# Loading the rows for block sums: one transfer over 96 partitions and one over 24, instead of four over 24

## The chip, the cores and the metric

The kernel runs on one core of one Trainium2 chip. The metric is the device time of one execution in microseconds (us), lower is better. The five engines are named as in the profile: PE (matrix multiplication), DVE (vector), ACT (scalar, activation), POOL (GpSimd) and SP (which only issues transfers and waits). All transfers between HBM and SBUF are carried by 16 DMA engines; SP and ACT issue theirs on hardware queues (q1 and q10 in the profile), POOL on a software queue (q0).

## The reference

Two layers one after the other, for 4 batches, 8 heads, 768 positions and 64 numbers a head, all in fp32.

```python
# layer 1: sparse attention (block=32, window=16)
k_sum = k.reshape(B, H, 24, 32, D).max(axis=3)
v_sum = v.reshape(B, H, 24, 32, D).mean(axis=3)      # the block sums of this case
scores = concat(local scores within the window, q.k_sum + log(32))
attn   = softmax(scores) @ concat([v, v_sum], axis=2)
# layer 2: mixture of 4 attention experts over x = attn in (B, S, 512)
w = softmax over the 2 best of x @ w_gate
out = sum over experts of w_e * (causal_attention(x wq_e, x wk_e, x wv_e) @ wo_e)
```

What matters here is `v_sum`: for every head, 24 sums of 32 consecutive rows of 64 numbers.

## The kernel before

The work is cut into batches `b` (0 to 3) and, inside a batch, into two groups `g` of four heads and four pairs `c` of two heads. Layer 1 works pair by pair (`stage1_pair`): transposes of q and k on PE, scores, an exponential on ACT (tile `aT`), the product with `vb` on PE (L437), division and transposes. Layer 2 (`stage2`) follows for each batch: projections (L630 with `wqk`, L554 with `wvg`), causal scores (L654), an exponential on ACT (L662, tile `a`), masking of the diagonal on POOL (L667), the product with v on PE (L678), and the output product (L734) with its stores (L745).

The order of the work is written out by hand: a table lists each step with its engine and its buffers, and every engine runs its steps strictly in that order. Neither the order nor the buffers change here.

The rows of v come to the core twice. The step `load_v` (SP, L284 to L287, four transfers a pair) lays the rows out in `vb`, 64 rows a tile, for the product. The block sums come in two ways. Three of the eight (batch, group) sets use PE (L304). The other five, (1,1), (2,0), (2,1), (3,0) and (3,1), use the function `tree`:

- Step `dvs` loads the rows of four heads into the tile `vt`, of which there is **one** buffer. Head j goes to partitions 32j to 32j+23: each partition holds one block of 32 rows, 2048 numbers, 8 KB, in one piece. These are four transfers on SP (L339), each 24 partitions by 8 KB.
- Two steps `tr` add on POOL (L347), in place: 2048 columns to 1024, then 512, 256, 128 and last 64 into the tile `vu`, over partitions 0 to 119. That is five additions for a set.
- Steps `ds` copy the sums from `vu` into `vb` (L170, by POOL).

Because `vt` has one buffer, the next set's load waits until POOL has made the last addition of the set before (SP's wait at L339 for `vu`). POOL's queue holds, behind the additions, the masks of layer 2 (L667) and the issues of the loads of k and q (L261, L266, tiles `kn` and `qn`), so whatever holds up an addition holds up these too. SP's queue holds, behind a `vt` load, the weights (L501, L507, L512; only behind the first), the `vb` loads and the output stores.

Each transfer on SP tells of its end by one of eight semaphores taken in turn, so a transfer isn't issued before the one eight places ahead has landed.

Of the kernel before, what the change touches and what calls it, by code (L numbers as in the profile page):

```python
# [7 lines left out]
FP32 = mybir.dt.float32  # L8
HALF = mybir.dt.float16
AL = mybir.AluOpType  # L10
# [5 lines left out]
S = 768  # L16
D = 64
# [5 lines left out]
NSUM = 24  # L23
# [135 lines left out]
def make_plan(nc, T, q, k, v, moe_w_gate, moe_wq, moe_wk, moe_wv, moe_wo, out):  # L159
# [3 lines left out]
    def en(e):  # L163
        return getattr(nc, ENG[e])

    def copy(e, dst, src):
        if e == "A":
            nc.scalar.copy(dst, src)  # L168
        else:
            en(e).tensor_copy(dst, src)  # L170
# [163 lines left out]
    def tree(b, g):  # L334
        t, u = R.buf("vt"), R.buf("vu")

        def load(e):
            for j in range(4):
                nc.sync.dma_start(out=T["vt"][t.slot][32 * j:32 * j + NSUM, :],  # L339
                                  in_=v[b, 4 * g + j].rearrange("(n s) d -> n (s d)", s=32))  # L340
        R.step(f"dvs{b}{g}", {"S": 1.8}, [vtz], [t], load, dma=3.0)
        for i, ws in enumerate(((1024,), (512, 256, 128, 64))):
            def add(e, ws=ws):
                x = T["vt"][t.slot]
                for w in ws:
                    y = T["vu"][u.slot] if w == 64 else x[:, 0:w]
                    en(e).tensor_tensor(y[0:120], x[0:120, 0:w], x[0:120, w:2 * w], AL.add)  # L347
            R.step(f"tr{b}{g}{i}", {"G": sum(0.13 + w * 0.00218 for w in ws)}, [t],
                   [u] if i else [t], add, keep=[t])
        for c in (2 * g, 2 * g + 1):  # L350
            def dsum(e, c=c):
                for h in range(2):
                    j = 32 * (2 * (c % 2) + h)
                    copy(e, T["vb"][vb[b, c].slot][WIN:KR, 12 * h:12 * h + 12, 0:64],
                         T["vu"][u.slot][j:j + NSUM, :].unsqueeze(1).to_broadcast((NSUM, NQ, 64)))
            R.step(f"ds{b}{c}", {"G": 1.75, "V": 0.95, "A": 1.64}, [u], [vb[b, c]], dsum)
# [403 lines left out]
    for i in range(24):  # L760
        fb, n = R.buf("ps"), 4 if i < 8 else 1
# [37 lines left out]
def decode(text):  # L799
    out = []  # L800
    for w in text.split():
        i, e, s = w.split(",")
        out.append((int(i) if i != "f" else -1, e, [int(x) for x in s.split(".") if x]))
    return out


@with_exitstack
def kernel(
    ctx: ExitStack,
    tc: tile.TileContext,  # L810
    q, k, v,
    moe_w_gate, moe_wq, moe_wk, moe_wv, moe_wo,
    out,
):
    nc = tc.nc
    ctx.enter_context(tc.manual_schedule())
    sb = ctx.enter_context(tc.tile_pool(name="sb", bufs=1))
    ps = ctx.enter_context(tc.tile_pool(name="ps", bufs=1, space=bass.MemoryType.PSUM))
    T = {}

    def one(name, shape, dt):
        T[name] = sb.tile(shape, dt, name=name)

    def many(name, shape, dt):
        T[name] = [sb.tile(shape, dt, name=f"{name}{i}") for i in range(SLOTS[name])]

    one("zz", (128, 512), HALF)
    one("w1", (128, 1), FP32)
    one("w1b", (128, 1), FP32)
    one("id16", (128, 128), HALF)  # L830
    one("idr", (KP, KP), HALF)
    one("id32", (128, 128), FP32)
    one("mt", (128, 128), HALF)
    one("pi", (128, 6, 64), HALF)
    one("wqk", (128, 2, NCH, 2, 128), HALF)
    one("wvg", (128, NCH, 264), HALF)
    one("wo", (128, 2, 512), HALF)
    one("wg32", (128, NCH, 4), FP32)
    one("wgt", (128, NCH, 4), FP32)
    many("qn", (128, 4, 384), HALF)  # L840
    one("sel", (96, 56), FP32)
    many("kn", (KP, 4, 512), HALF)
    many("ks", (128, NSUM), HALF)
    many("kw", (128, NQ, 128), HALF)
    many("qT", (128, S), HALF)
    many("aT", (128, 2, 384), FP32)
    many("x32", (128, S), FP32)
    many("vb", (128, 24, 65), FP32)
    many("vs", (128, 2, 128), FP32)
    many("vt", (128, 2048), FP32)  # L850
    many("vu", (128, 64), FP32)
    many("rec", (128, 2, NT, 1), FP32)
    many("hi", (128, S), HALF)
    many("lo", (128, S), HALF)
    many("v2", (128, NT, E, 65), HALF)
    many("lgp", (128, NT, 4), FP32)
    many("gt", (128, 6, NT, 4), FP32)
    many("qk", (128, S), HALF)
    many("a2", (128, 5376), HALF)
    many("cmb", (128, 2, NT, 1), FP32)  # L860
    many("wav", (128, NT, 128), HALF)
    many("wT", (128, S), HALF)
    one("ob", (128, SLOTS["ob"], 512), FP32)
    T["ps"] = ps.tile((128, 8, 512), FP32, name="ps")
    T["ps16"] = T["ps"].bitcast(HALF)

    R = make_plan(nc, T, q, k, v, moe_w_gate, moe_wq, moe_wk, moe_wv, moe_wo, out)
    R.emit(decode(TABLE))
# [30 lines left out]
```

## Time and profile before

| | us |
|---|---|
| median of 3 runs | 167.77 (167.38 to 168.11) |
| the profiled execution | 168.57 |
| its span, first to last instruction | 166.7 |

The profile covers the one execution of 168.57 us; 1.9 us of it lie outside the span. Its page gives busy time by engine, a row of digits for 40 slices of the span, the DMA queues, the chain of work that ended last, groups of instructions, and the transfers by the line that issued them. Times in views are us from the start of the span. A bracket at the end of a timeline row tells how long the engine was idle before it and what ended that. In the view by stretches (windows), the last three numbers are the granted PE clock as a fraction, the mean busy share of the 16 DMA engines (it can exceed 1, as packets overlap) and GB/s.

### The profile page before, as it was taken

The numbers are of one execution on the slowest core, as the hardware profiler recorded it, in microseconds if no ns is written. First come the engines' busy times: TensorE is split into PE (matmuls) and PEld (weight loads), VectorE is DVE, ScalarE is ACT, GpSimd is POOL, SyncE is SP. The second block draws the span as 40 slices with busy tenths as digits, with TensorE's granted clock in tenths as the row PEclk, the third lists the DMA queues.
The fourth block names the chain that finished last, engine by engine and source line by source line (L and its number), as shares of the span: only waits on it lengthen the run. The fifth ranks groups of instructions, "written<-read, shape, count | busy, mean of one in ns | idle before, by whom it ended". The sixth has DMA issues, their size and how long they took to land.

```text
span 166.7 us, 6783 instructions
## 1 busy us (share of the span) xinstructions
PE 144.8 (87%) x2903; PEld 107.5 (64%) x2903; DVE 114.7 (69%) x235; ACT 123.9 (74%) x159; POOL 111.5 (67%) x181
## 2 busy tenths in 40 slices
PE   0259798996899979995999989999999999999993
PEld 0246676873677757684757878766678795477551
DVE  5074389869586885964986879993974797247840
ACT  3048976998499968996779877797877874997630
POOL 7988699628998588799699999716999130315000
DMA  3999999999988996999798958998400000200572
GB/s 28 170 215 227 217 209 155 233 215 166 174 212 174 135 202 135 167 186 179 178 142 117 257 102 222 200 219 294 175 4 6 0 4 4 114 11 22 231 283 102
DMA packets 44302, 25.35 MB, mean 152 GB/s; under 512 B 33168, under 2 KB 40592, under 8 KB 43792
## 3 DMA queue, kind: packets, MB, share of 16 engines
q1 hardware_dynamic: 35840, 17.96, 48.2%
q0 software_dynamic: 7488, 6.29, 25.7%
q10 hardware_dynamic: 944, 0.66, 1.2%
q8 instruction: 23, 0.38, 1.1%
q14 instruction: 7, 0.06, 0.1%
HBM read 24.91 MB, written 6.29 MB: 187 GB/s over the span
## 4 chain that ended last, share of the span: by engine, by line
PE 48%; DMA 20%; DVE 11%; ACT 6%; issue 6%; POOL 5%; SPq 2%; POOLq 0%; DVEq 0%; ACTq 0%
DMA qn<-in_q_dram 9%; PE ps L437 9%; PE ps L630 6%; DMA out_dram<-ob 6%; DMA kn<-in_k_dram 5%; PE ps L554 5%; PE ps L366 4%; PE ps L734 4%; PE ps L678 4%; PE ps L654 4%; PE ps L304 3%; PE ps L766 3%; PE ps L414 2%; ACT a L662 2%; DVE x L452 2%
## 5 line engine op out<-in xcount | busy, mean ns | idle before, releaser
L662 ACT ACTIVATE a<-ps 128x1024 f16<-128x1024 f32 (+1 forms) x48 | 42.2, 921 | 7.2 <-PE ps L654 6.0
L667 POOL TENSOR_SCALAR_AFFINE_SELECT a<-a 128x256 f16<-128x256 f16 x48 | 18.7, 408 | 20.8 <-ACT a L662 20.1
L427 ACT ACTIVATE aT<-ps 120x768 f32<-120x768 f32 x32 | 25.3, 817 | 6.8 <-PE ps L420 6.7
L437 PE MATMUL ps<-vb,aT 120*64 120x65 f32 x768 | 26.5, 224 | 1.3 <-issue 0.7
L347 POOL TENSOR_TENSOR vt<-vt 120x1024 f32<-120x1024 f32 (+3 forms) x20 | 24.0, 1202 | 4.9 <-DMA vt<-in_v_dram 3.8
L437 PEld LDWEIGHTS ps<-vb,aT 120*64 120x64 f32 x768 | 24.1, 138 | 4.3 <-issue 2.3
L630 PE MATMUL ps<-hi,wqk 128*128 128x384 f16 x128 | 23.1, 326 | 2.2 <-issue 1.9
L630 PEld LDWEIGHTS <-wqk 128*128 128x128 f16 x128 | 11.9, 98 | 10.8 <-issue 2.9
L170 POOL COPY vb<-vb 32x1408 f32<-32x1408 f32 x10 | 13.4, 1350 | 6.0 <-PE ps L734 4.4
L482 DVE TENSOR_TENSOR lo<-ps,hi 128x768 f16<-128x768 f32 x16 | 15.2, 955 | 2.9 <-ACT hi L168 2.4
L170 POOL COPY vb<-vu 24x768 f32<-24x768 f32 x20 | 16.5, 823 | 1.1
L366 PE MATMUL ps<-idr,kn 100*64 100x100 f16 x256 | 8.9, 219 | 9.4 <-POOL kn L219 7.4
L452 DVE TENSOR_TENSOR x<-ps,rec 128x768 f32<-128x768 f32 x16 | 15.3, 958 | 0.6
L382 DVE TENSOR_REDUCE ks<-ps 128x24 f16<-128x768 f16 x16 | 15.1, 952 | 0.4
L170 DVE COPY kw<-ps 128x1152 f16<-128x1152 f16 x8 | 10.8, 1353 | 6.5 <-PE ps L366 6.5
L654 PE MATMUL ps<-qk,qk 64*128 64x512 f16 (+3 forms) x128 | 14.8, 307 | 0.6 <-ACT qk L168 0.3
L168 ACT COPY vb<-vb 32x1408 f32<-32x1408 f32 x6 | 8.0, 1361 | 8.5 <-DMA vb<-in_v_dram 8.4
L366 PEld LDWEIGHTS <-kn 100*64 100x64 f16 x256 | 7.2, 117 | 10.4 <-POOL kn L219 7.4
L554 PE MATMUL ps<-wvg,hi 128*128 128x264 f16 x96 | 13.8, 275 | 0.0
L168 ACT COPY qT<-ps 128x768 f16<-128x768 f16 x13 | 10.4, 801 | 2.7 <-PE ps L366 2.7
L678 PEld LDWEIGHTS <-a 128*128 128x128 f16 x336 | 11.1, 97 | 1.9 <-issue 1.0
L420 PEld LDWEIGHTS <-kw 64*128 64x128 f16 x384 | 10.4, 98 | 2.9 <-issue 0.7
(97 smaller groups left out, 282.7 us busy)
## 6 DMA issues: line engine op xcount, KB each, us to landing
vb<-in_v_dram SPq DMA_DIRECT2D x32, 176.0 KB
out_dram<-ob SPq DMA_DIRECT2D x10, 512.0 KB
vt<-in_v_dram SPq DMA_DIRECT2D x20, 192.0 KB
kn<-in_k_dram POOLq DMA_DIRECT2D x6, 384.0 KB, 8.2
qn<-in_q_dram POOLq DMA_DIRECT2D x6, 384.0 KB, 6.2
kn<-in_k_dram POOLq DMA_DIRECT2D x4, 192.0 KB, 4.9
qn<-in_q_dram POOLq DMA_DIRECT2D x4, 192.0 KB, 6.3
a<-in_moe_wk_dram SPq DMA_DIRECT2D x2, 256.0 KB
```

Of the source, the lines that this page charges most:

```text
L168: nc.scalar.copy(dst, src)
L170: en(e).tensor_copy(dst, src)
L347: en(e).tensor_tensor(y[0:120], x[0:120, 0:w], x[0:120, w:2 * w], AL.add)
L366: nc.tensor.transpose(dst[64 * hp:64 * hp + 64, p * s:p * s + p], src[:, hh + hp, 64 * s:64 * s + 64], idt)
L427: nc.scalar.activation(T["aT"][aT.slot][0:KR], pbank(sc, 2)[0:KR, :, 0:384], AF.Exp, scale=SCALE)
L437: nc.tensor.matmul(pbank(av, 2)[o:o + 64, u, 65 * (2 * (t // 2) + hp):65 * (2 * (t // 2) + hp) + 65], a[0:KR, hp, 64 * t:64 * t + 64], T[" ...
L452: nc.vector.tensor_tensor(T["x32"][x32.slot].rearrange("p (u t w) -> p u t w", u=2, w=64), avv()[:, :, :, 0:64], T["rec"][rec.slot].to_bro ...
L554: nc.tensor.matmul(p[:, i, 0:264], hi_(ch)[:, cols], T["wvg"][:, ch, :], start=(ch == 0), stop=False, skip_group_check=True)
L630: nc.tensor.matmul(pbank(pp, 2)[:, u, 0:384], T["wqk"][:, cc, ch, j, :], hi_(ch)[:, 384 * u:384 * u + 384], start=(ch == 0), stop=(ch == N ...
L654: nc.tensor.matmul(pbank(sp, 2)[:, ep, c0:c0 + w], T["qk"][qk[1].slot][r, 128 * tj:128 * tj + 128], T["qk"][qk[0].slot][r, n0:n0 + w], sta ...
L662: nc.scalar.activation(a2v(u), pbank(sp, 2)[:, :, 0:ln], AF.Exp, scale=SCALE / (XS * XS))
L667: nc.gpsimd.affine_select(m, m, [[0, 2], [1, 128]], AL.is_ge, 0.0, base=0, channel_multiplier=-1)
```

## The change

The four transfers of a set become two. The first has 96 destination partitions: the first 24 of each group of 32 partitions take the 24 blocks of a head, as before; the other 8 take the first 8 blocks of the next head, which no one uses. In HBM that is an access pattern of 3 heads (step S*D), 32 blocks a head (step 2048 numbers), 4 pieces a block, 512 numbers a piece. The second transfer loads the fourth head to partitions 96 to 119. The tile gets a row of 4 by 520 numbers instead of 2048, so that a block lies as four pieces of 512 numbers (2 KB) with a gap of 32 bytes after each. The additions run over the same numbers through views of two, then one piece. As the program carries it, the first transfer's HBM side has the counts 3, 128, 512 and its SBUF side 96, 4, 512. Bytes read for a set: 96 rows of 8 KB for the first transfer (786 KB) and 197 KB for the second, against four times 197 KB (786 KB) before. All other instructions, and their order on every engine, stay.

```diff
         def load(e):
-            for j in range(4):
-                nc.sync.dma_start(out=T["vt"][t.slot][32 * j:32 * j + NSUM, :],
-                                  in_=v[b, 4 * g + j].rearrange("(n s) d -> n (s d)", s=32))
+            x, y = T["vt"][t.slot], v[b, 4 * g]
+            nc.sync.dma_start(out=x[0:96, :, 0:512],
+                              in_=bass.AP(y.tensor, y.offset, [[S * D, 3], [2048, 32], [512, 4], [1, 512]]))
+            nc.sync.dma_start(out=x[96:96 + NSUM, :, 0:512],
+                              in_=v[b, 4 * g + 3].rearrange("(n w s) d -> n w (s d)", w=4, s=8))
...
                 for w in ws:
-                    y = T["vu"][u.slot] if w == 64 else x[:, 0:w]
-                    en(e).tensor_tensor(y[0:120], x[0:120, 0:w], x[0:120, w:2 * w], AL.add)
+                    if w == 1024:
+                        y, a0, a1 = x[:, 0:2, 0:512], x[:, 0:2, 0:512], x[:, 2:4, 0:512]
+                    elif w == 512:
+                        y, a0, a1 = x[:, 0, 0:512], x[:, 0, 0:512], x[:, 1, 0:512]
+                    else:
+                        a0, a1 = x[:, 0, 0:w], x[:, 0, w:2 * w]
+                        y = T["vu"][u.slot] if w == 64 else a0
+                    en(e).tensor_tensor(y[0:120], a0[0:120], a1[0:120], AL.add)
...
-    many("vt", (128, 2048), FP32)
+    many("vt", (128, 4, 520), FP32)
```

## The prediction

> **What bounds the kernel now.** I read the page first (busy shares, the slices, the queues, the issues), then the waits of SP's queue, then the timelines of SP and POOL around the five `vt` loads, and last two stretches of the DMA load.
>
> ```profile
> span 166.7 us, 6783 instructions
> PE 144.8 (87%) x2903; PEld 107.5 (64%) x2903; DVE 114.7 (69%) x235; ACT 123.9 (74%) x159; POOL 111.5 (67%) x181
> DMA  3999999999988996999798958998400000200572
> q1 hardware_dynamic: 35840, 17.96, 48.2%
> L347 POOL TENSOR_TENSOR vt<-vt 120x1024 f32<-120x1024 f32 (+3 forms) x20 | 24.0, 1202 | 4.9 <-DMA vt<-in_v_dram 3.8
> vt<-in_v_dram SPq DMA_DIRECT2D x20, 192.0 KB
> ```
>
> No engine is full over the whole span. PE, the busiest, is at 87%, but up to about 120 us (slice 28 of 40) the DMA engines are near full too. The five sets of block sums fall in just that part. The row for L347 says that POOL already stood idle for 3.8 us because a `vt` load wasn't there.
>
> ```profile
> SPq L339 <- POOL vu L347: 6.9, 2, 3.6
> 31.58 1.54 SPq L339 DMA_DIRECT2D vt<-in_v_dram  x4
> 34.23 6.98 SPq L507 DMA_DIRECT2D a<-in_moe_wv_dram  x2
> 48.86 2.25 SPq L339 DMA_DIRECT2D vt<-in_v_dram  x4
> 64.33 2.12 SPq L339 DMA_DIRECT2D vt<-in_v_dram  x4
> 78.10 2.44 SPq L339 DMA_DIRECT2D vt<-in_v_dram  x4
> 105.43 1.59 SPq L339 DMA_DIRECT2D vt<-in_v_dram  x4
> ```
>
> ```profile
> 41.01 2.34 POOL L347 TENSOR_TENSOR vt<-vt 120x1024 f32<-120x1024 f32 x1
> 47.12 0.32 POOL L347 TENSOR_TENSOR vu<-vt 120x64 f32<-120x64 f32 x1
> 58.85 5.05 POOL L347 TENSOR_TENSOR vt<-vt 120x1024 f32<-120x1024 f32 x4 [2.39 <-DMA vt<-in_v_dram]
> 63.98 0.32 POOL L347 TENSOR_TENSOR vu<-vt 120x64 f32<-120x64 f32 x1
> 72.65 5.03 POOL L347 TENSOR_TENSOR vt<-vt 120x1024 f32<-120x1024 f32 x4
> 77.75 0.32 POOL L347 TENSOR_TENSOR vu<-vt 120x64 f32<-120x64 f32 x1
> 88.35 2.37 POOL L347 TENSOR_TENSOR vt<-vt 120x1024 f32<-120x1024 f32 x1
> 115.48 2.35 POOL L347 TENSOR_TENSOR vt<-vt 120x1024 f32<-120x1024 f32 x1 [1.38 <-DMA vt<-in_v_dram]
> ```
>
> These two views are a ring. A set's additions end (64.30), the next load is issued at once (64.33), its rows are there about 8 us later, POOL adds (72.65), the additions end (78.07), the next load goes out (78.10). From issue to first addition the five sets take 9.43, 9.99, 8.32, 10.25 and 10.05 us. With one buffer nothing in this ring can overlap, so a longer load lengthens it directly. Sets 2 and 5 wait for the load already. At the others POOL was just in time: the shortest, 8.32, bounds what a load needs, so the slack of sets 1 and 4 is at most 1.1 and 1.9 us, together 3.0.
>
> Whether a late POOL matters is read from who comes next:
>
> ```profile
> 69.45 0.77 POOL L667 TENSOR_SCALAR_AFFINE_SELECT a<-a 128x256 f16<-128x256 f16 x2
> 70.98 1.44 PE L678 MATMUL ps<-v,a 128*128 128x65 f16 x42
> 123.70 1.48 POOL L667 TENSOR_SCALAR_AFFINE_SELECT a<-a 128x256 f16<-128x256 f16 x4
> 125.23 1.21 PE L678 MATMUL ps<-v,a 128*128 128x65 f16 x34
> ```
>
> The masks behind the second set end at 70.22 and PE's L678 starts at 70.98; behind the fifth it is 125.18 and 125.23. PE has 0.05 to 0.8 us in hand, so POOL's delay is PE's delay, in an order that is fixed.
>
> **The load, part by part.** How is a transfer shared among the 16 DMA engines? The page's q1 row gives 35,840 packets. The program's pieces on SP are 24,576 runs for `vb`, 6,144 for the weights wq, wk and wv, 256 for wo, 2,816 for the output and 480 for `vt` (20 loads of 24 rows), 34,272 in all. The 1,568 that remain are marks of completion, one for each engine that a transfer uses: 83 other transfers by 16 is 1,328, and 240 are left for 20 `vt` loads, 12 each. So 24 rows ran on 12 engines, the largest number up to 16 that divides 24. All of these transfers have the same outermost count on both sides. [...] My forecast is that the first load runs on 3 engines, a head each. [...]
>
> At what pace? The two nearest rows:
>
> ```profile
> 52.00:54.00 2.00, 2.00 (x21) 0.97 (x18) 0.89 (x1) 1.90 (x3) 2.00 (x4) 1.00 0.81 164
> 160.00:162.50 2.50, 2.50 (x15) 1.30 (x14) 0.42 (x1) 0.86 (x2) 0.00 (x0) 1.00 1.00 368
> ```
>
> In the first stretch the second `vt` load moves with little else beside it: 164 GB/s, over 12 engines 13.7 GB/s each. In the second, the output's 2 KB pieces go over all 16: 368 GB/s, 23 GB/s each. Before, a set is 786 KB at 164 GB/s, 4.8 us. After, each of the three engines carries 262 KB, and then 16 KB of the fourth head (197 KB on 12 engines), 278 KB: at 13.7 GB/s 20.3 us, at 23 GB/s 12.1 us. A set gets longer by 15.5 or by 7.3 us.
>
> I take the slower pace, because that row is the same tile, the same queue and the same direction; the 23 GB/s are stores. [...]
>
> Five sets by 15.5 are 77.5 us. Taken off: 3.0 for the slack of sets 1 and 4. Then the queue ahead: of load 3's 8.32 us, 8.32 − 4.8 = 3.5 are queue and latency; while POOL stands still the queue drains, so I take half of that off the four later loads, 7 us. That leaves 67.5. About an eighth (8 us, an estimate) I give back because engines that hinder each other can drift apart over 128 pieces of 2 KB, which two pieces of 8 KB a load don't allow. The sum is 60 us: 168.57 + 60 = 228.6 for an execution like the profiled one, which is 0.8 above the median shown; so 228. The same sum at the fast pace is 5 × 7.3 = 36.5, less 3 and nothing else, 33: 201.
>
> **The rest of the change.** Two issues on SP instead of four: the load rows above show 1.54 to 2.44 us for four, so at most 1 to 1.2 us a set are saved on SP. It is worth nothing, because SP is held anyway. After the first load the two L507 issues take 6.98 us: the queue takes no more until the pieces ahead are gone. With 128 pieces on each of three engines it is held for most of the 20 us, and the weights, the `vb` loads and, behind set 5, three output stores stand behind it, though 13 engines are free. I price this at nothing beside the ring, since POOL stands still for the same time; if POOL were not held, this is what would be late next (the `wqk` casts after set 1 need weights behind the load). The additions have the same element counts, so 24.0 us of L347 stay; a tenth more for the two-piece view of the first (2.34) would be 1.2 us over five. A quarter more bytes for `vt` (197 KB a set) is contained in the 262 KB. The small pieces could help the k and q loads of POOL's queue, which now alternate with pieces of 8 KB; the chain holds two of these:
>
> ```profile
> 53.53 8.70 DMA qn<-in_q_dram
> 68.74 9.14 DMA kn<-in_k_dram
> ```
>
> Both are issued behind a set's additions and before the next set's. Three of their engines would be shared with the long load, so they gain nothing and may lose; bounds −3 to +5 us over the kernel, taken as 0.
>
> **The rivals.** *Three engines at full pace.* If each engine runs at the 23 GB/s of the output stores, the time is 201. For it: pieces of 2 KB ran at this pace in that row, and three engines load HBM little. Against: every `vt` load so far ran at 13.7.
>
> *Sixteen engines.* If the split goes by the 96 rows of SBUF alone, 786 KB at 368 GB/s take 2.1 us and the fourth head 197 KB at 164 GB/s 1.2: 3.3 instead of 4.8. Only the two waits that the L347 rows show can shrink, 1.5 of 2.39 and 1.38 of 1.38, so 2.9 us: 165. It decides from about nine engines up (786 KB / (9 × 23 GB/s) = 3.8, and 0.7 to 1.2 for the fourth head, makes 4.8). This is the case that ends on the other side. Against it: the 12 for 24 rows shows that the split follows counts of the pattern, and 3 is one. [...]
>
> *Late, but half hidden.* PE, ACT and DVE go on while POOL waits, and the later sets' sums are used late. If half of the fast sum is hidden, 168 + 17 = 185. Against it: 0.05 to 0.8 us between masks and L678.
>
> **How the numbers follow.** Three engines at the slow pace 0.60 (its own range 212 to 242: the 60 us less a quarter, and the 67.5 plus 7 for k and q and for the additions); three at full pace 0.25 (194 to 211); half hidden 0.06; sixteen engines 0.09, of which 0.07 faster by over 0.5% and 0.02 within 0.5%. Half a per cent is about what a measurement of this kernel can tell from no change. The first two cases hold 0.85, so the range goes from 194 to 242.
>
> **What would show it.** Right: five idle times of POOL ahead of L347, each 10 us or more, released by the `vt` load; DMA share in these stretches near 0.2 to 0.4 with GB/s well under 164; marks on q1 that come to 15 for a set (3 and 12); SP's issues behind a load held for over 10 us; the additions as long as before. Step by step: 20 us from issue to landing confirm the slow pace, 12 to 13 the fast one. Wrong: 11 or more marks for the first load, or L347's idle time under 4 us in all.

## The result, and the profile after

| | before | after |
|---|---|---|
| median, us | 167.57 (166.56 to 168.11, 4 runs) | 231.88 (230.5 to 234.09, 4 runs) |
| profiled execution, us | 168.57 | 234.09 |
| its span, us | 166.7 | 232.4 |

The kernel became slower by a factor of 1.382 (95% interval 1.370 to 1.394), 64.3 us in the medians. The profiled execution after is 2.2 us above its median, the one before 1.0 above its own. Ratios with an interval, here and below, compare fast executions alone, those within 1.5% of the fastest of their kernel.

From the page after: the span, the busy shares, the row of PE's granted clock, q1, the chain by engine, the additions, and the issues of the `vt` rows and of k and q. Lines after L339 are eight higher than before: the additions are L355, the masks L675, PE's product with v L686. The second transfer of a set is issued at L341.

```profile
span 232.4 us, 6770 instructions
PE 159.6 (69%) x2903; PEld 117.1 (50%) x2903; DVE 114.6 (49%) x235; ACT 125.0 (54%) x159; POOL 111.6 (48%) x181
PEclk9999999985799599597975759689995589999999
q1 hardware_dynamic: 37595, 18.95, 32.1%
DMA 47%; PE 19%; POOL 17%; DVE 4%; SPq 4%; ACT 3%; issue 3%; POOLq 0%; DVEq 0%; ACTq 0%
L355 POOL TENSOR_TENSOR vt<-vt 120x1024 f32<-120x1024 f32 (+3 forms) x20 | 24.0, 1200 | 71.7 <-DMA vt<-in_v_dram 70.7
vt<-in_v_dram SPq DMA_DIRECT2D x5, 768.0 KB
kn<-in_k_dram POOLq DMA_DIRECT2D x6, 384.0 KB, 10.3
qn<-in_q_dram POOLq DMA_DIRECT2D x6, 384.0 KB, 10.8
```

POOL has the same 111.6 us of work as before (111.5), the additions the same 24.0, but it stood 70.7 us for the rows, against 3.8. The difference, 66.9 us, covers the whole of what the span grew (65.7). The chain that ended last, in which DMA and PE had other shares before (20% and 48%), is now 47% DMA.

The chain in order of time names the stretches. First number the start, second the length:

```profile
33.73 18.67 DMA vt<-in_v_dram
60.38 23.03 DMA vt<-in_v_dram
89.85 22.69 DMA vt<-in_v_dram
119.01 22.93 DMA vt<-in_v_dram
158.12 6.34 SPq L341
164.52 15.30 DMA out_dram<-ob
```

Four of the five loads lie on it in full. For the fifth it goes by SP's second issue of the set, held for 6.34 us, and an output store that stands behind the load. POOL's timeline at the five first additions, and SP's at the loads and at what stood behind two of them:

```profile
52.58 2.34 POOL L355 TENSOR_TENSOR vt<-vt 120x1024 f32<-120x1024 f32 x1 [8.82 <-DMA vt<-in_v_dram]
83.54 5.05 POOL L355 TENSOR_TENSOR vt<-vt 120x1024 f32<-120x1024 f32 x4 [15.21 <-DMA vt<-in_v_dram]
112.71 5.05 POOL L355 TENSOR_TENSOR vt<-vt 120x1024 f32<-120x1024 f32 x4 [16.97 <-DMA vt<-in_v_dram]
142.09 2.35 POOL L355 TENSOR_TENSOR vt<-vt 120x1024 f32<-120x1024 f32 x1 [15.10 <-DMA vt<-in_v_dram]
178.72 2.34 POOL L355 TENSOR_TENSOR vt<-vt 120x1024 f32<-120x1024 f32 x1 [14.62 <-DMA vt<-in_v_dram]
```

```profile
32.82 0.86 SPq L339 DMA_DIRECT2D vt<-in_v_dram  x1
33.73 4.64 SPq L341 DMA_DIRECT2D vt<-in_v_dram  x1
59.54 0.79 SPq L339 DMA_DIRECT2D vt<-in_v_dram  x1
66.51 10.65 SPq L286 DMA_DIRECT2D vb<-in_v_dram  x2
89.02 0.79 SPq L339 DMA_DIRECT2D vt<-in_v_dram  x1
118.18 0.79 SPq L339 DMA_DIRECT2D vt<-in_v_dram  x1
124.50 11.69 SPq L286 DMA_DIRECT2D vb<-in_v_dram  x2
157.27 0.80 SPq L339 DMA_DIRECT2D vt<-in_v_dram  x1
```

From issue to first addition the five sets take 19.8, 24.0, 23.7, 23.9 and 21.5 us: 112.8 in all, against 48.0 before, 64.8 more. The time grew by the same 64.3 us, so the ring of load and additions passed its whole growth on to the end.

How many engines carried the first load is read from the q1 row. The program's pieces on SP are 33,792 besides `vt` (24,576 + 6,144 + 256 + 2,816) and 480 a set, 2,400: 36,192. The row has 37,595, so 1,403 marks are left; the trace's records of single packets have just 1,403 of 4 bytes on this queue. The 83 other transfers make 1,328; the 75 that remain are 15 a set, 12 for the 24 rows of the fourth head and 3 for the large load. It ran on three engines.

Two stretches inside loads, in the view by stretches, show what that looks like (last three numbers: PE's granted clock, DMA share, GB/s):

```profile
42.50:47.50 5.00, 5.00 (x126) 3.80 (x126) 5.00 (x5) 4.34 (x7) 1.25 (x1) 1.00 0.21 63
132.00:137.00 5.00, 1.03 (x20) 1.03 (x22) 0.00 (x0) 0.14 (x1) 0.00 (x0) 0.59 0.22 56
```

A share of 0.21 is 3.4 engines of 16, which agrees with three marks for the large load. In the first stretch almost only the long load moves: 63 GB/s, some 20 GB/s for each of three engines. In the second PE works 1.03 of 5 us and the other compute engines next to nothing, but the load isn't alone. The records of single packets have 100 pieces of 2 KB there (96 ns each in the median) and 98 of 768 B (78 ns), which are pieces of a load of q.

### The profile page after: what moved, and what is told of

Same layout as the page of the kernel before. It is cut to its first block, busy times and chain, and to the rows that moved or that the text cites. A ratio compares the mean times of both kernels' runs of the same rounds, so it can differ in the third digit from the quotient of the medians.

```text
span 232.4 us, 6770 instructions
## 1 busy us (share of the span) xinstructions
PE 159.6 (69%) x2903; PEld 117.1 (50%) x2903; DVE 114.6 (49%) x235; ACT 125.0 (54%) x159; POOL 111.6 (48%) x181
## 3 DMA queue, kind: packets, MB, share of 16 engines
q1 hardware_dynamic: 37595, 18.95, 32.1%
## 4 chain that ended last, share of the span: by engine, by line
DMA 47%; PE 19%; POOL 17%; DVE 4%; SPq 4%; ACT 3%; issue 3%; POOLq 0%; DVEq 0%; ACTq 0%
DMA vt<-in_v_dram 38%; POOL vt L355 8%; DMA out_dram<-ob 7%; PE ps L445 4%; DMA qn<-in_q_dram 3%; POOL vb L170 3%; SPq L341 3%; PE ps L562 2%; PE ps L686 2%; PE ps L774 2%; ACT a L670 2%; PE ps L742 2%; PE ps L304 1%; PE ps L662 1%; POOL a L675 1%
## 5 line engine op out<-in xcount | busy, mean ns | idle before, releaser
L355 POOL TENSOR_TENSOR vt<-vt 120x1024 f32<-120x1024 f32 (+3 forms) x20 | 24.0, 1200 | 71.7 <-DMA vt<-in_v_dram 70.7
L675 POOL TENSOR_SCALAR_AFFINE_SELECT a<-a 128x256 f16<-128x256 f16 x48 | 18.7, 410 | 22.7 <-ACT a L670 21.9
L445 PE MATMUL ps<-vb,aT 120*64 120x65 f32 x768 | 27.9, 231 | 1.1 <-POOL vb L170 1.0
L686 PE MATMUL ps<-v,a 128*128 128x65 f16 x336 | 16.1, 212 | 18.2 <-POOL a L675 18.0
L445 PEld LDWEIGHTS ps<-vb,aT 120*64 120x64 f32 x768 | 25.6, 145 | 4.6 <-issue 2.0
L686 PEld LDWEIGHTS <-a 128*128 128x128 f16 x336 | 14.1, 109 | 21.3 <-POOL a L675 19.5
L562 PE MATMUL ps<-wvg,hi 128*128 128x264 f16 x96 | 18.2, 334 | 9.6 <-ACT wvg L168 9.5
L662 PE MATMUL ps<-qk,qk 64*128 64x512 f16 (+3 forms) x128 | 16.9, 343 | 10.6 <-DVE ob L170 10.1
L374 PE MATMUL ps<-id,qn 128*64 128x128 f16 x192 | 9.6, 250 | 16.1 <-DMA qn<-in_q_dram 16.1
L374 PEld LDWEIGHTS <-qn 128*64 128x64 f16 x192 | 7.2, 127 | 17.6 <-DMA qn<-in_q_dram 17.0
L562 PEld LDWEIGHTS <-hi 128*128 128x128 f16 x96 | 9.2, 110 | 13.1 <-issue 10.5
L705 DVE RECIPROCAL ps<-ps 128x12 f32<-128x12 f32 (+2 forms) x10 | 2.2, 222 | 27.1 <-PE ps L686 27.1
## 6 DMA issues: line engine op xcount, KB each, us to landing
kn<-in_k_dram POOLq DMA_DIRECT2D x6, 384.0 KB, 10.3
qn<-in_q_dram POOLq DMA_DIRECT2D x6, 384.0 KB, 10.8
```

Source lines behind the costliest of these rows:

```text
L355: en(e).tensor_tensor(y[0:120], a0[0:120], a1[0:120], AL.add)
L374: nc.tensor.transpose(dst[64 * hp:64 * hp + 64, p * s:p * s + p], src[:, hh + hp, 64 * s:64 * s + 64], idt)
L445: nc.tensor.matmul(pbank(av, 2)[o:o + 64, u, 65 * (2 * (t // 2) + hp):65 * (2 * (t // 2) + hp) + 65], a[0:KR, hp, 64 * t:64 * t + 64], T[" ...
L562: nc.tensor.matmul(p[:, i, 0:264], hi_(ch)[:, cols], T["wvg"][:, ch, :], start=(ch == 0), stop=False, skip_group_check=True)
L662: nc.tensor.matmul(pbank(sp, 2)[:, ep, c0:c0 + w], T["qk"][qk[1].slot][r, 128 * tj:128 * tj + 128], T["qk"][qk[0].slot][r, n0:n0 + w], sta ...
L675: nc.gpsimd.affine_select(m, m, [[0, 2], [1, 128]], AL.is_ge, 0.0, base=0, channel_multiplier=-1)
```

## The experiments

**The same load with 96 as outermost count in HBM** (e1_hbm96).

```diff
-                              in_=bass.AP(y.tensor, y.offset, [[S * D, 3], [2048, 32], [512, 4], [1, 512]]))
+                              in_=bass.AP(y.tensor, y.offset, [[2048, 96], [512, 4], [1, 512]]))
```

> The changed kernel, with one thing different: the first load reads 96 blocks that follow one another in HBM (outermost count 96, then 4 pieces of 2 KB) instead of 3 heads of 32. Bytes, pieces, the SBUF side, the number of transfers and the order stay; what differs in the output is that the partitions hold other blocks, so the sums are those of the wrong blocks. Theory (the common divisor of both sides' outermost counts, 3, put the load on three engines): now 16 engines share it, about 3.3 us a set, POOL's idle time ahead of its first additions falls from 70.7 us to under 6, and the time is 164 to 169 us. Rival (the extra quarter of bytes, the 2 KB pieces, or one large transfer as such makes it slow): the time stays above 220 us.

Measured: 168.42 us, ratio to before 1.003 (0.999 to 1.008). Its q1 row and its additions:

```profile
q1 hardware_dynamic: 37660, 18.95, 50.4%
L355 POOL TENSOR_TENSOR vt<-vt 120x1024 f32<-120x1024 f32 (+3 forms) x20 | 24.1, 1204 | 4.8 <-DMA vt<-in_v_dram 3.7
```

37,660 packets are 65 more than in the changed kernel, 13 a set: 16 engines for the large load instead of 3. With the same bytes, pieces, tile and issues, all 64 us are gone. So the extra quarter of bytes, the 2 KB pieces and the large transfer as such cost nothing that shows; the outermost count of 3 on the HBM side was the cause. (One more thing differs: the changed kernel reads 8 blocks of each next head a second time, this run doesn't. The run with 32 partitions a head, further below, reads them twice too and is not slower.) It also shows what the change could have brought had it spread: nothing (POOL's wait for the rows is 3.7 us, as before 3.8).

**Four loads with pieces of 2 KB** (e2_four_2kb).

```diff
-            nc.sync.dma_start(out=x[0:96, :, 0:512], ...)
-            nc.sync.dma_start(out=x[96:96 + NSUM, :, 0:512], ...)
+            for j in range(4):
+                nc.sync.dma_start(out=x[32 * j:32 * j + NSUM, :, 0:512],
+                                  in_=v[b, 4 * g + j].rearrange("(n w s) d -> n w (s d)", w=4, s=8))
```

> The changed kernel with its tile of 4 by 520 and 2 KB pieces, but the four transfers of 24 partitions from before, a head each, so 12 engines each. Theory (the number of engines is all that matters): the time of the kernel before, 166 to 169 us; the additions in their two-piece form as long as before, 2.34 us. If the 8 KB pieces held up the loads of k and q in POOL's queue, up to 3 us faster, 164 to 166. Rival (pieces of 2 KB or the padded tile cost something themselves): slower than 170 us.

Measured: 167.34 us, ratio 0.997 (0.992 to 1.002). No difference from before: the pieces and the padded tile cost nothing that shows, and the hoped-for help to the loads of k and q does not show. The first addition takes 2.35 to 2.38 us in its two-piece form, against 2.34 to 2.37.

**Two heads in one load, over partitions 0 to 63 or 32 to 95** (e3_heads01, e4_heads12). The first:

```diff
-            nc.sync.dma_start(out=x[0:96, :, 0:512], in_=<3 heads>)
-            nc.sync.dma_start(out=x[96:96 + NSUM, :, 0:512], in_=<head 3>)
+            nc.sync.dma_start(out=x[0:64, :, 0:512],      # the other run: x[32:96], heads 1 and 2
+                              in_=bass.AP(y.tensor, y.offset + 0 * S * D, [[S * D, 2], [2048, 32], [512, 4], [1, 512]]))
+            for j in (2, 3):                              # the other run: (0, 3)
+                nc.sync.dma_start(out=x[32 * j:32 * j + NSUM, :, 0:512], in_=<head j>)
```

> Heads 0 and 1 of a set in one load over partitions 0 to 63 (outermost counts 2 and 64), heads 2 and 3 in two loads of 24 partitions. Theory of the engines: 2 engines with 128 pieces of 2 KB each. [...] Rival (no hindrance between engines, each at 84 to 95 ns a piece): 11 to 12 us for the pieces, and 200 to 212 us in all.

> The same as the run with heads 0 and 1 in one load, but heads 1 and 2 in one load over partitions 32 to 95, and heads 0 and 3 in two loads of 24 partitions. Same number of engines (2), pieces, bytes and distance in HBM. [...] Rival (the hindrance is in HBM, whose distance between the two streams is the same here, or there is none): the same time as with heads 0 and 1 within 4 us.

Measured, one run each: 236.03 us with heads 0 and 1, 222.81 with heads 1 and 2. Both have 37,490 packets on q1; the pieces are 33,792 + 5 × (256 + 192) = 36,032 and 1,458 marks are left, less 1,328 is 26 a set: 12, 12 and 2. So two heads run on two engines. POOL's and SP's rows for the first and the fifth set, heads 0 and 1:

```profile
32.66 0.65 SPq L339 DMA_DIRECT2D vt<-in_v_dram  x1
52.44 2.34 POOL L356 TENSOR_TENSOR vt<-vt 120x1024 f32<-120x1024 f32 x1 [9.70 <-DMA vt<-in_v_dram]
158.91 0.58 SPq L339 DMA_DIRECT2D vt<-in_v_dram  x1
180.64 2.35 POOL L356 TENSOR_TENSOR vt<-vt 120x1024 f32<-120x1024 f32 x1 [15.28 <-DMA vt<-in_v_dram]
```

Heads 1 and 2:

```profile
32.51 0.76 SPq L339 DMA_DIRECT2D vt<-in_v_dram  x1
50.13 2.34 POOL L356 TENSOR_TENSOR vt<-vt 120x1024 f32<-120x1024 f32 x1 [7.54 <-DMA vt<-in_v_dram]
150.96 0.70 SPq L339 DMA_DIRECT2D vt<-in_v_dram  x1
168.44 2.34 POOL L356 TENSOR_TENSOR vt<-vt 120x1024 f32<-120x1024 f32 x1 [11.01 <-DMA vt<-in_v_dram]
```

From issue to addition: 19.8 and 21.7 against 17.6 and 17.5. Over all five sets it is 114.5 against 101.5, 13.0 us, which is the difference in time (13.2); four executions of the changed kernel lie within 3.6 us. The two loads have the same number of engines and pieces and the same distance in HBM; what differs is the partitions, and which heads are read.

How the paces differ is seen in stretches in which only pieces of the two-head load move (last number GB/s), three with heads 0 and 1:

```profile
62.40:65.20 2.80, 2.80 (x67) 2.29 (x64) 1.71 (x3) 1.73 (x3) 1.81 (x4) 0.85 0.13 32
123.20:124.50 1.30, 0.00 (x0) 0.00 (x0) 0.00 (x0) 0.00 (x0) 1.22 (x5) 0.50 0.13 47
163.20:164.70 1.50, 1.49 (x40) 1.21 (x33) 1.42 (x3) 1.48 (x4) 1.45 (x3) 1.00 0.13 27
```

Then three with heads 1 and 2:

```profile
43.00:46.00 3.00, 3.00 (x105) 2.64 (x106) 3.00 (x4) 2.67 (x4) 0.00 (x0) 1.00 0.13 49
60.40:62.40 2.00, 2.00 (x55) 1.53 (x52) 1.40 (x3) 1.41 (x3) 0.98 (x4) 1.00 0.13 51
115.30:118.00 2.70, 0.51 (x10) 0.52 (x11) 0.00 (x0) 0.00 (x0) 2.62 (x6) 0.50 0.13 47
```

In these, heads 1 and 2 go at 47 to 51 GB/s. Heads 0 and 1 go at the same pace for a while and at little more than half of it (27 to 32) for a while. Heads 0 and 1 take longer in all five sets (by 1.3 to 4.2 us), which lie at five places in HBM; that the place of the heads has no part in it was not tried by itself. What slows the two engines no run shows. Over a whole set the loss is small, 2.6 us, because the pace is cut only part of the time. In size the forecasts missed: two engines that hinder each other were put at 222 to 234 us, two that don't at 200 to 212, some 20 us less. 236.03 and 222.81 lie above these, and they are 13 us apart. The rival of the second run, the same time within 4 us, falls.

**Two buffers** (e5_two_buffers).

```diff
-SLOTS = dict(..., vs=2, vt=1, ...)
+SLOTS = dict(..., vs=2, vt=2, ...)
...
+            if st.name.startswith("dvs"):
+                sets += 1
+                slots = [sets % 2]
```

> The changed kernel with two buffers for the tile of the rows, used in turn, so that a load no longer waits for the additions of the set before it. Theory (the time is the length of the load on three engines; SP is held behind it, so a second buffer only lets SP issue a load as soon as it comes to it): SP stood 4.7 and 5.0 us at two of the five loads, so 8 to 10 us less than the changed kernel, 220 to 225 us. Rival (the ring of one buffer alone makes it slow, and with a second one the loads hide behind other work): under 200 us.

Measured, one run: 219.59 us, 12.3 less than the changed kernel, just under the 220 to 225 of the theory. POOL still stands 58.6 us for the rows:

```profile
L358 POOL TENSOR_TENSOR vt<-vt 120x1024 f32<-120x1024 f32 (+3 forms) x20 | 24.0, 1199 | 59.6 <-DMA vt<-in_v_dram 58.6
```

The one buffer is about a fifth of the 64 us. From issue to addition the five sets take 17.8 to 25.1 us, and SP is held behind the load (10.30 to 12.97 us for two `vb` issues behind each of sets 2, 3 and 4), so a load issued earlier is still not early enough.

**Half of the pieces** (e6_half_pieces).

```diff
-            nc.sync.dma_start(out=x[0:96, :, 0:512],
-                              in_=bass.AP(y.tensor, y.offset, [[S * D, 3], [2048, 32], [512, 4], [1, 512]]))
+            nc.sync.dma_start(out=x[0:96, 0:2, 0:512],
+                              in_=bass.AP(y.tensor, y.offset, [[S * D, 3], [1024, 32], [512, 2], [1, 512]]))
```

> The changed kernel with half of the pieces in the first load: 3 heads of 32 partitions with 2 pieces of 2 KB each, 64 pieces an engine instead of 128; half of the columns of the first three heads are left unloaded, so their sums are wrong. Theory (each piece on the three engines lengthens the kernel by its own time): 64 pieces at 97 to 135 ns are 6 to 8.6 us a set, so 31 to 43 us less over five sets: 188 to 201 us. Rival (a fixed cost of a three-engine transfer or of the long issue on SP): above 215 us.

Measured, one run: 181.25 us, 50.6 less than the changed kernel, more than the 31 to 43 expected. The first and the last load and their additions, with SP's second issue:

```profile
31.99 0.87 SPq L339 DMA_DIRECT2D vt<-in_v_dram  x1
32.90 0.84 SPq L341 DMA_DIRECT2D vt<-in_v_dram  x1
44.46 2.37 POOL L355 TENSOR_TENSOR vt<-vt 120x1024 f32<-120x1024 f32 x1
116.59 0.80 SPq L339 DMA_DIRECT2D vt<-in_v_dram  x1
128.60 2.35 POOL L355 TENSOR_TENSOR vt<-vt 120x1024 f32<-120x1024 f32 x1 [4.79 <-DMA vt<-in_v_dram]
```

From issue to addition it takes 12.5, 13.0, 14.0, 12.5 and 12.0 us, 64.0 in all: 48.8 less than the changed kernel, for 320 pieces fewer on each of the three engines. That is 152 ns a piece, k and q loads beside them included. With 64 pieces an engine SP's second issue takes 0.84 us; with 128 it took 4.64 and 6.34 us (the L341 rows above). So this issue is held behind 128 pieces on each of three engines and not behind 64; what holds it no run shows.

**Loads of 32 partitions, with one and with two buffers** (e7_rows32, e8_rows32_two). Both start from the kernel before, to see whether anything beats it.

```diff
             for j in range(4):
-                nc.sync.dma_start(out=T["vt"][t.slot][32 * j:32 * j + NSUM, :],
-                                  in_=v[b, 4 * g + j].rearrange("(n s) d -> n (s d)", s=32))
+                r, y = 32 if j < 3 else NSUM, v[b, 4 * g + j]
+                nc.sync.dma_start(out=T["vt"][t.slot][32 * j:32 * j + r, :],
+                                  in_=bass.AP(y.tensor, y.offset, [[2048, r], [1, 2048]]))
...
-        for t in T["vt"]:
-            en(e).memset(t, 0.0)
+        pass
```

> The kernel before with loads of 32 partitions for the first three heads of a set (8 blocks of the next head beside the 24) and of 24 for the fourth, 8 KB pieces as before, and without the first clearing of the tile, which nothing reads any more. 32 rows go over 16 engines, as 2 rows each. [...]

> The same as the run with 32 partitions a head, with two buffers for the rows, used in turn. Theory: POOL's waits for the load (2.39 and 1.38 us in the kernel before) and SP's for the additions (6.9) go, but the loads then come earlier among the loads of k and q: 2 to 4 us less than before, 163.5 to 166. Rival (DMA engines bound this stretch, so an earlier load only delays the others): 166 to 169.

Measured, as ratios to before: 0.993 (0.986 to 1.000) with one buffer, which can't be told from no change; 1.011 (1.004 to 1.017) with two, slower by a per cent, against the expectation and on the side of its rival. For the first, 165.5 to 167.7 us had been expected, since the clearing (1.81 us of POOL) and SP's wait of 3.1 us for it go; how many engines its loads of 32 rows took no row here shows. Each ratio rests on three of twelve executions. With two buffers POOL still stands 3.5 us for the rows, against 3.8 before. So an earlier load brings nothing here, and no version found beats the kernel before. Why the second is slower was not followed further.

## Why the prediction was right, point by point

The forecast was 228 us (194 to 242), the measurement 231.88. By its steps:

- *Three engines.* Shown: 3 marks for the large load, and the time back at 168.42 us when only the HBM count changed. Sixteen engines, the rival on the other side, is what that run is; it would have been 168, not 165. What rules the number no run shows; the marks give 3 for 3 in HBM against 96 in SBUF, 16 for 96 against 96, 2 for 2 against 64 and 12 for 24 against 24.
- *The ring passes its growth on.* Shown: 64.8 us from issue to addition, 66.9 of POOL's waits, 64.3 in time. With half of the pieces 48.8 and 50.6. Nothing of it was hidden, so the rival of half hidden time falls. The prediction had all five of POOL's waits at 10 us or more; four are, the first is 8.82.
- *The pace.* Forecast 13.7 GB/s an engine, 150 ns for 2 KB. As an average over a set it holds: the slope over the pieces is 152 ns, and the 201 us that the rival at the full pace gave are too few. But it is not the pace of an engine. With almost nothing else moving, the three bring some 20 GB/s each (63 GB/s in 42.50:47.50), near the 23 of that rival. The prediction took the pace of the same tile, queue and direction, and put the step from the full pace to the slow one, 8.2 us a set, down to engines that hinder each other. No row of before shows that they do; the pair of runs with two heads in a load shows 2.6 us a set between its partitions, for two engines. The prediction's row of 164 GB/s also holds 160 pieces of 256 B, 20 of the 164, so the tile's own pace in it is 12 GB/s an engine rather than 13.7. That the total came within 4 us is therefore in part luck. The rest of the 8.2 comes from elsewhere:
- *The loads of k and q*, priced at 0 with bounds of −3 to +5 us. Their landing went from 8.2 and 6.2 us to 10.3 and 10.8. Two of them are issued during each of sets 2, 3 and 4, whose loads took 23.9 us on average, against 20.6 in sets 1 and 5: 3.3 more, near 10 us over three sets. The same pattern stands in the run with heads 1 and 2 (22.1 against 17.6). The packets of 132.00:137.00 show the sharing: 100 pieces of the long load to 98 of q, so that three engines bring a piece of the load in 150 ns each, though the piece itself takes 96. The records don't name the engine; that it is the same three is read from the share of 0.22, 3.5 engines. What k and q cost in all was not tried by itself, so the 10 us are an estimate from the five sets, and rather a low one: shortly before sets 1 and 5 one such load is issued too.
- *Taken together*: 36.5 us for the full pace on three engines, 13 for engines that slow each other (the difference of the pair, measured with two engines; that it holds for three is the author's estimate) and 10 for k and q make 59.5 of 64.8; some 5 us stay without a name. The prediction took off 7 us for a queue that drains, which no run shows, and 8 for engines that drift apart. A pace that changes is seen (47 and 27 GB/s within one run, with heads 0 and 1); that engines drift apart, and that this is worth 8 us, no run shows.
- *Issues, additions, bytes at nothing.* Shown by the two runs at 168.42 and 167.34 us. That SP is held was foreseen (10.65 and 11.69 us for two issues at L286) and priced at nothing beside the ring. It is not held until all the pieces ahead are gone: in the second set the two issues were through at 77.16, and POOL had the rows at 83.54. In the fifth set the chain does go through it (6.34 us).

## What to carry to other kernels

Before merging transfers, write down the outermost count of each side of the access pattern: here the numbers of engines were 12 for 24 rows, 16 for 96, 3 for 3 heads against 96 rows and 2 for 2 against 64. A transfer in fewer instructions can be one on fewer engines (here 3 instead of 12), and then it is long for everyone behind it on that queue (here 10.65 us for two `vb` issues). The packets of a queue, less the pieces that the program asks for, told here how many engines took part. And other queues' pieces can move beside a long load: here, with 98 pieces of q beside 100 of the load, three engines brought a piece of the load every 150 ns each, though it takes 96 itself.

## What was not expected

PE's granted clock fell. It is 1.00 in all the stretches shown of before, and in the stretches after it is 1.00 where PE is busy (42.50:47.50) and 0.59 where it works 1.03 of 5 us (132.00:137.00); the digits of the PEclk row go down to 5. PE's busy time grew by 14.8 us (144.8 to 159.6) for the same 2903 instructions. Why it fell no run shows. What it cost was not tried by itself. Little of it shows: POOL's longer waits alone make up the whole growth, and PE is 19% of the chain.
